# Where the first loads of x and of the key weights are issued, and new tables for the order, in a two-layer attention and gated-layer kernel

## The chip, the cores and the metric

The kernel runs on one core of a Trainium2 chip. The metric is the device time of one execution in microseconds (us); smaller is better. Engines are named TensorE (PE in the profile), VectorE (DVE), ScalarE (ACT), GpSimd (POOL) and SyncE (SP). PEld is TensorE's weight load.

## What is computed

The input x has 2048 rows of 512 values in bf16. Two blocks are applied in turn, and the pair is applied twice with the same weights:

```python
x = x + A(layernorm(x))     # attention, 32 heads of 16, causal window of 256 keys
x = x + B(layernorm(x))     # gated layer: (sigmoid(x @ w_gate) * (x @ w_up)) @ w_down, 1792 wide
x = x + A(layernorm(x))
x = x + B(layernorm(x))

def A(x):
    q, k, v = split(x @ wqkv)                      # per head
    s = (q @ k.T) / 4, where 0 <= i - j < 256
    return (softmax(s) @ v) @ wo
```

## The kernel before, in words

**Tiling.** Rows of x are cut into 16 tiles of 128 (`NT`), and four tiles make a group (`NTG` is 4 groups). All of x (`xsb`), all weights (`wq`, `wot`, `wg`, `wu`, `wd`) and all intermediate buffers lie in SBUF for the whole run. Within a tile, the rows lie in an interleaved manner over the partitions (two halves z of 64 rows), which is why one tile is loaded either as two DMAs of 64 partitions or as one DMA over a rearranged source.

**Stages of a tile.** The layer norm (`layer_norm`) takes statistics on VectorE (`stats`: L589, L590, and L592 for the first group), an inverse root on GpSimd (`root`: L598, L599) and applies both on VectorE (L617) into a buffer `xn`, of which there are two. The first tiles are transposed by TensorE (L638) and copied by ScalarE or VectorE (the shared helper `copy`, L666 on ScalarE and L668 on VectorE) into `xnT`; later tiles by a DMA transpose. Then `q_unit` (L703), `k_unit` (L734) and `v_unit` (L770) are matmuls with `wq`. The keys are evacuated (L666 or L668) and then split by a mask into even and odd heads on VectorE (L749, with `rms`). A visit of `scores` (L1029, L1040) writes four PSUM banks `Sps`, one exponential of 2048 columns on ScalarE (L1082) reads them into `PTring` or `edge`, VectorE multiplies masks in (L960), and `values` (L1109) multiplies with the values in `Vaug` and with copies of them, `Vl` and `Vh`, in which the two halves of a tile are swapped to other partitions and the rest is zero. Those copies are made by SP's DMAs (L1314, `half_values`). `zeros(z, i)` clears the rest of a copy (L534, GpSimd). After the values come the normalisation, the output projection (`oproj_unit`, L893, added to x at L899), the second norm, the gate and up projections (`glu_units`, L798, with a tanh at L816 and a product at L824) and the down projection (`down_units`, L862, added at L871). Rows of the result go out by SP's DMAs (L878).

**How the order is made.** No loop order is written down. While the program is built, a planner (`Plan`) plays the engines forward with costs in nanoseconds. Each piece of work is a task with its engine or a choice of engines, what it waits for, and a priority; whenever an engine is free in the plan, the ready task of lowest priority number is put next into that engine's instruction stream. TensorE's next piece is chosen by `pick` and `rank`: a score visit when the pace allows (`PACE`), else values, else a unit of matmuls. The tables `PRIO`, `SLACK`, `RANK` and their `LATE_` forms, `PACE` and `OPT` are plain numbers that set this order; `EXP_NS`, `SWITCH`, `COLD`, `RATE`, `LAND` and the like are what the planner believes of the hardware. On the chip, each engine runs its stream in that order, and semaphores hold an instruction until its inputs are there. The planner's numbers therefore change the order and nothing else.

**The gated layer's groups.** `GLU[0][OPT["g0"]]` and `GLU[1][OPT["g2"]]` say how many tiles of a layer share one pass over gate and up weights. A group of n tiles makes matmuls of n x 128 columns. In layer 0 both kernels use 1, 1, 1, 1, 2, 2, 4, 4.

**The first loads.** `loads` issues, on the queues SP and ACT, each tile of x as two halves: tile 0, tile 1, tiles 2 and 3; then the key weights, the query weights (each as two halves), and the value weights on ACT; then, on SP, tiles 4 to 7, `wot`, tiles 8 to 11, `wg`, `wu` and the rest (issues at L455). `constants` runs before that on GpSimd and VectorE: the identity for the transposes (L507, L508), parts of the value buffers (`ones`, L528 and L529), the masks `rms`, and the clears of `Vl`. `later_constants` makes masks, the clears of `Vh` and the rest as tasks of the plan. `keep_warm` (L1292) puts four matmuls on the identity into TensorE's stream where nothing else is ready.

Of the kernel before, what the change touches and what calls it, by code (L numbers as in the profile page):

```python
# [12 lines left out]
P = 128  # L13
S, D, H, DH, F = 2048, 512, 32, 16, 1792
# [42 lines left out]
def pool_ns(n):  # L57
# [4 lines left out]
TAIL = (384, 128)  # L62
GLU = [[[1] * 4 + [4], [1] * 4 + [2] * 2, [1] * 6 + [2], [1] * 8, [2] * 4, [1] * 2 + [2] * 3, [2] * 2 + [4]], [[4] * 3 + [2, 1, 1], [4] * 3 + [2, 2], [4] * 4]]
PACE = [2682, 3207, 1600, 2511, 23.52]
EARLY = 12
FILL = 800
# [3 lines left out]
PE_LATENCY = 180  # L70
COLD = 5200
SWITCH = 96
LAND = 1230
RATE = ((3300, 330.0), (5300, 160.0), (1e9, 345.0))
FIRST = 1100
# [5 lines left out]

PRIO = dict(st_x0=7.13, ap_x0=2.72, xt_x0=3.36, st_x1=-0.44, ap_x1=1.86, xt_x1=6.58, st_x=18.87, ap_x=6.56,
    xt_x=2.0, st_p=7.13, ap_p=4.46, xt_p=0.81, st_g=2.23, ap_g=1.32, xt_g=6.14, st_g0=5.97, ap_g0=3.21,
    xt_g0=1.33, tp=5.75, tp_g=-0.06, q=4.0, q0=5.51, q1=4.74, k=1.95, k0=-0.89, k1=-1.49, s=-1.15, s0=5.46,
    s1=3.28, v=0.28, v0=5.43, v1=14.72, vv=5.53, exp=3.64, exp0=4.71, m0=4.61, m00=-0.56, e0=1.11, e00=1.28,
    e1=7.21, e10=6.56, m2=0.64, m20=3.6, th=5.12, mu=-0.12, dn=1.29, add=-0.27, add0=1.8, out=-2.4, mv=5.8,
    mv0=6.23, oq=-2.27, oq0=-0.14, no=4.71, no0=2.61, on=5.93, on0=0.59, vc=9.2, vc0=-0.87)
OPT = dict(gu='SP', g1=1, bk=3, bq=2, wide=0, r0=2, g0=1, g2=1, x0=1, eps=1, hold=0, own=1, ck=0, cq=2,
    turn=2)
SLACK = dict(xt=1208, oq=843, on=211, vc=1208)  # L90
RANK = dict(tp=-1.708, o=-2, lead=14.747, far=7.411, v=9.3, g=1.778, d=1.823, feed=11.672, x3=21097, wd=474,
    go=364)
LATE_PRIO = dict(st_p=-0.04, ap_p=7.96, xt_p=-0.99, st_x=1.07, ap_x=4.81, xt_x=-1.16, st_g=1.75, ap_g=1.19,
    xt_g=2.76, q=3.84, k=4.33, s=4.05, v=0.61, exp=1.12, m0=4.62, e0=2.79, e1=4.39, m2=5.49, th=1.65, mu=2.51,
    dn=2.1, add=0.69, out=0.45, mv=3.49, oq=0.77, no=6.44, on=2.16, vc=0.22)
LATE_SLACK = dict(xt=489, oq=1327, on=2346, vc=897)
LATE_RANK = dict(tp=-2, o=1.576, lead=9.722, far=6.159, v=1.796, g=1.769, d=3.896, feed=7.551, go=1418)

# [69 lines left out]
class Plan:  # L168
# [20 lines left out]
    def at(self, time, fn=None):  # L189
        self.seq += 1  # L190
        heapq.heappush(self.heap, (time, self.seq, fn))
# [177 lines left out]
class Net:  # L369
# [74 lines left out]
    def loads(self, A_x, wqkv, wo, w_gate, w_up, w_down):  # L444
# [26 lines left out]
        def both(parts):  # L471
            done = Event()
            when_all(parts, done.fire)
            return done

        for t, n in {1: ((0, 1), (1, 1), (2, 2)), 2: ((0, 2), (2, 2)), 3: ((0, 1), (1, 3))}[OPT["x0"]]:
            ev = load_x(self.xsb[:, t:t + n, :], slice(t, t + n), n, 0, ("SP", "ACT"))
            for i in range(t, t + n):
                self.has_x[i] = ev
        if OPT["wide"]:  # L480
            self.has_wq["q"] = self.has_wq["k"] = both([
                load(self.wq[:, k:k + 2, 0:2 * D], wq_src[:, k:k + 2, 0:2 * D], 4 * P * D * 2, prio=0, queue=q, row=4 * D)
                for k, q in ((0, "ACT"), (2, "SP"))])
        else:
            for w in "kq":
                h = slice("qk".index(w) * D, ("qk".index(w) + 1) * D)
                self.has_wq[w] = both([load(self.wq[:, k:k + 2, h], wq_src[:, k:k + 2, h], 2 * P * D * 2, prio=0, queue=q)
                                       for k, q in ((0, "ACT"), (2, "SP"))])
        self.has_wq["v"] = load(self.wq[:, :, 2 * D:3 * D], wq_src[:, :, 2 * D:3 * D], D * D * 2, prio=0, queue="ACT")
        x_group(1)  # L490
# [12 lines left out]

    def constants(self):
        nc = self.nc
        nc.gpsimd.memset(self.nhalf[:], -0.5)
        nc.gpsimd.memset(self.ident[:], 0.0)  # L507
        nc.gpsimd.affine_select(out=self.ident[:], in_=self.ident[:], compare_op=ALU.not_equal, fill=1.0,  # L508
                                base=0, pattern=[[-1, P]], channel_multiplier=1)
        for i in range(2):  # L510
            self.ones(i, nc.vector)
        nc.vector.memset(self.rms[0][:], 0.0)
        for m in range(4):
            nc.vector.memset(self.rms[0][32 * m:32 * m + 16, :], 1.0)
        nc.vector.tensor_scalar(out=self.rms[1][:], in0=self.rms[0][:], scalar1=-1.0, scalar2=1.0,
                                op0=ALU.mult, op1=ALU.add)
        for i in range(2):
            self.zeros(0, i)
        self.pl.free["POOL"] = 3000.0
        self.pl.free["SP"] = self.pl.free["ACT"] = 750.0  # L520
        self.pl.at(750.0)
        self.pl.at(1500.0)
        self.pl.free["DVE"] = 3600.0
        self.pl.at(3600.0)

# [10 lines left out]
    def later_constants(self):  # L536
# [11 lines left out]
        def mask2(e):  # L548
            for z in range(2):
# [8 lines left out]
                                    op0=ALU.mult, op1=ALU.add)  # L558

        for i in range(2):  # L560
            self.vzero[i] = pl.task({"POOL": 800}, lambda e, i=i: self.zeros(1, i), first, prio=8, port=True).done
# [7 lines left out]
    def layer_norm(self, key, t, deps):  # L569
# [50 lines left out]
        if key == ("p", 0, 0) and t >= 2 and OPT["hold"]:  # L620
            deps = deps + [self.applied[t - 2]]
        a = pl.task({"DVE": 910 + 70 * first}, stats, deps, self.prio["st_" + kind], lambda: "st" in box or self.has("st"))
        if not alone:
# [378 lines left out]
    def scores(self, L, t, kind, i):  # L1002
# [5 lines left out]
        if kind == "A":  # L1008
# [23 lines left out]
            runs = cut  # L1032
            return pl.count(8 * len(runs)) or 220
        if kind == "R":
            zs = range(2 if t + 2 < NT else 1)
            for z in zs:
                for cq in range(NCQ):
                    q0, o = ((L * NT + t) * 2 + 5 * z) % (QG * TGW // HP) * HP, (z * NCQ + cq) * HP
                    for m in range(4):
# [3 lines left out]
                                         start=True, stop=True, tile_position=(32 * m, 0))  # L1043
            return pl.count(16 * len(zs)) or 122 * len(zs)
        for cq in range(NCQ):
            for e in range(2):
                o = (2 * cq + e) * HP
                q0 = ((L * NT + t) * 2 + 1) % (QG * TGW // HP) * HP
                for m in range(4):
                    nc.tensor.matmul(self.sps[:, m, o:o + HP], lhsT=kTp[32 * m:32 * m + 32, cq, tt, e, :],  # L1050
                                     rhs=self.qT[32 * m:32 * m + 32, cq, q0:q0 + HP],
                                     start=True, stop=True, tile_position=(32 * m, 0))
        return pl.count(32) or 230

# [29 lines left out]
    def values(self, L, t, half, bank):  # L1084
# [7 lines left out]
        for col in range(4):  # L1092
# [10 lines left out]
            for k, (where, Va, p) in enumerate(parts):  # L1103
# [8 lines left out]
                pl.count(4)  # L1112
        return n * 56

# [173 lines left out]
    def keep_warm(self, bank):  # L1288

        nc, pl = self.nc, self.pl  # L1290
        for i in range(4):
            nc.tensor.matmul(self.banks[bank][:, 0:P], lhsT=self.ident[:], rhs=self.ident[:], start=True, stop=True)  # L1292
        pl.count(4)
        pl.matmul("d", 4 * 56)
# [8 lines left out]
    def half_values(self):  # L1303
# [18 lines left out]
        for z in range(2):  # L1322
            some = pairs if z == 0 else [k for k in pairs if k[1] + 2 < NT]
            for i, (L, t) in enumerate(some):
                V = self.Vaug[(L * NT + t) // 2 % VP]
                deps = [self.v_ready[L, t], self.v_ready[L, t + 1]]
                if z and i < 2:
                    deps.append(self.vzero[i])
                if i >= 2:
# [83 lines left out]
    def go(self, *srcs):  # L1413
# [28 lines left out]
        self.pv_list = [k + (h,) for k in LT for h in range(2)]  # L1442
        self.constants()
        self.loads(*srcs)
        self.streams = [[], [], [], [], []]
        self.roots, self.pairs, self.vones, self.vzero = {}, {}, {}, {}
        self.applied = [Event() for _ in range(NBG)]
# [74 lines left out]
```

The softmax here doesn't subtract the row's maximum and nothing guards it: scores larger than these inputs give would overflow.

## Time and profile before

| | |
|---|---|
| median of 3 runs | 541.69 us (541.08 to 543.02) |
| span of the profiled execution, first to last instruction | 539.6 us |
| what the median has beyond that span | 2.1 us |
| TensorE busy, instructions | 531.1 us, 9658 matmuls |
| VectorE busy | 420.5 us |
| ScalarE busy | 382.3 us |
| GpSimd busy | 43.4 us |
| mean granted TensorE clock | 0.999 |

The profile gives the span of one execution; for that execution no other total is given, so the median of the runs stands beside it. Busy time of a pipelined engine counts as busy whatever overlaps, so 98% on TensorE doesn't say that it works at its peak. In the timeline a row with a count (x10) joins instructions of one kind that follow one another; its length runs from the first start to the last end. What stands in square brackets is the engine's idle time before it and what ended that.

### The profile page before, as it was taken

The numbers are of one execution on the slowest core, as the hardware profiler recorded it, in microseconds if no ns is written. First come the engines' busy times: TensorE is split into PE (matmuls) and PEld (weight loads), VectorE is DVE, ScalarE is ACT, GpSimd is POOL, SyncE is SP. The second block draws the span as 40 slices with busy tenths as digits, with TensorE's granted clock in tenths as the row PEclk, the third lists the DMA queues.
The fourth block names the chain that finished last, engine by engine and source line by source line (L and its number), as shares of the span: only waits on it lengthen the run. The fifth ranks groups of instructions, "written<-read, shape, count | busy, mean of one in ns | idle before, by whom it ended". The sixth has DMA issues, their size and how long they took to land.

```text
span 539.6 us, 21359 instructions
## 1 busy us (share of the span) xinstructions
PE 531.1 (98%) x9658; PEld 293.0 (54%) x9658; DVE 420.5 (78%) x844; ACT 382.3 (71%) x380; POOL 43.4 (8%) x99
## 2 busy tenths in 40 slices
PE   8999999999999999999999999999999999999997
PEld 8446755855767444544444444544444444455873
DVE  6999999789878997798977789778677785674442
ACT  4989989878888687776778767787667866540330
POOL 5301110001000110101100010101000000000000
PEclk9999999999999999999999999999999999999999
DMA  8890334232421323143110622117211241132001
GB/s 260 317 227 15 43 72 57 50 61 63 72 52 33 72 51 60 36 101 59 32 35 14 105 51 47 38 42 108 54 45 28 60 72 50 24 70 58 2 11 39
DMA packets 95067, 36.23 MB, mean 67 GB/s; under 512 B 78336, under 2 KB 93952, under 8 KB 94976
## 3 DMA queue, kind: packets, MB, share of 16 engines
q1 hardware_dynamic: 93600, 33.56, 29.9%
q8 instruction: 75, 1.23, 1.0%
q10 hardware_dynamic: 1376, 1.31, 0.8%
q14 instruction: 16, 0.13, 0.1%
HBM read 9.70 MB, written 2.10 MB: 22 GB/s over the span
## 4 chain that ended last, share of the span: by engine, by line
PE 89%; DVE 5%; ACT 2%; DMA 1%; issue 1%; POOL 0%; SPq 0%; ACTq 0%; POOLq 0%
PE bank L798 37%; PE bank L862 18%; PE bank L1109 9%; PE Sps L1029 7%; PE bank L893 5%; PE bank L734 4%; PE bank L770 3%; PE bank L703 3%; PE Sps L1040 2%; ACT PTring L1082 1%; DMA wq<-in_A_wqkv_dram 1%; DVE kTp L749 1%; DVE st L589 1%; DVE PTring L960 1%; DVE edge L960 1%
## 5 line engine op out<-in xcount | busy, mean ns | idle before, releaser
L1082 ACT ACTIVATE PTring<-Sps 128x2048 bf16<-128x2048 f32 (+1 forms) x122 | 226.0, 1852 | 63.2 <-PE Sps L1029 59.2
L798 PE MATMUL bank<-xnT,wu 128*128 128x512 bf16 (+2 forms) x728 | 128.2, 297 | 0.0
L798 PE MATMUL bank<-xnT,wg 128*128 128x512 bf16 (+2 forms) x728 | 128.2, 298 | 0.0
L862 PE MATMUL bank<-wd,hT 128*128 128x512 bf16 (+2 forms) x462 | 109.9, 373 | 0.0
L824 DVE SCALAR_TENSOR_TENSOR hT<-hT,bank 128x256 bf16<-128x256 bf16 (+1 forms) x154 | 80.8, 537 | 34.0 <-ACT hT L816 21.2
L816 ACT ACTIVATE hT<-bank 128x256 bf16<-128x256 f32 (+1 forms) x154 | 71.1, 482 | 48.5 <-PE bank L798 47.8
L798 PEld LDWEIGHTS <-wg 128*128 128x128 bf16 x728 | 60.7, 98 | 36.7 <-issue 2.3
L798 PEld LDWEIGHTS <-wu 128*128 128x128 bf16 x728 | 61.4, 98 | 34.5 <-issue 2.5
L1082 ACT ACTIVATE edge<-Sps 128x2048 bf16<-128x2048 f32 (+1 forms) x32 | 56.6, 1770 | 17.3 <-PE Sps L1040 17.3
L862 PEld LDWEIGHTS <-hT 128*128 128x128 bf16 x462 | 43.0, 98 | 46.4 <-issue 2.2
L668 DVE CAST OTs<-bank 128x512 bf16<-128x512 f32 x59 | 43.0, 729 | 21.5 <-PE bank L1109 21.1
L960 DVE TENSOR_TENSOR PTring<-PTring,mask 128x1024 bf16<-128x1024 bf16 x64 | 43.7, 684 | 12.3 <-ACT PTring L1082 12.1
L1109 PE MATMUL bank<-PTring,Vaug 128*32 128x64 bf16 (+1 forms) x2880 | 52.0, 203 | 0.0
L1109 PEld LDWEIGHTS <-Vaug 128*32 128x32 bf16 x2880 | 44.0, 97 | 12.0 <-issue 10.4
L1029 PE MATMUL Sps<-qT,kTp 32*128 32x256 bf16 (+3 forms) x1216 | 47.4, 248 | 1.2 <-ACT PTring L1082 1.1
L598 POOL TENSOR_SCALAR st<-st 128x2 f32<-128x2 f32 (+1 forms) x33 | 10.7, 325 | 443.6 <-DVE st L590 443.6
L589 DVE BATCH_NORM_STATS2 st<-xsb 128x6 f32<-128x512 bf16 x64 | 43.9, 686 | 1.7 <-DMA xsb<-in_A_x_dram 1.2
L1109 PE MATMUL bank<-edge,Vl 128*32 128x64 bf16 x1024 | 44.4, 193 | 0.1
L960 DVE TENSOR_TENSOR edge<-edge,maske 128x1024 bf16<-128x1024 bf16 x60 | 40.3, 682 | 3.4 <-ACT edge L1082 3.3
L1029 PEld LDWEIGHTS <-kTp 32*128 32x128 bf16 x1216 | 18.2, 92 | 45.4 <-issue 43.5
L1109 PE MATMUL bank<-edge,Vh 128*32 128x64 bf16 x896 | 40.8, 193 | 0.0
L960 DVE TENSOR_TENSOR PTring<-PTring,maskn 128x1024 bf16<-128x1024 bf16 x56 | 38.2, 682 | 0.0
(73 smaller groups left out, 522.0 us busy)
## 6 DMA issues: line engine op xcount, KB each, us to landing
Vl<-Vaug SPq DMA_DIRECT2D x32, 68.0 KB, 2.4
out_dram<-xsb SPq DMA_DIRECT2D x15, 128.0 KB, 2.1
Vh<-Vaug SPq DMA_DIRECT2D x28, 68.0 KB, 2.5
wg<-in_B_w_gate_dram SPq DMA_DIRECT2D x2, 896.0 KB, 9.7
wu<-in_B_w_up_dram SPq DMA_DIRECT2D x2, 896.0 KB
wd<-in_B_w_down_dram SPq DMA_DIRECT2D x7, 256.0 KB, 5.3
xsb<-in_A_x_dram SPq DMA_DIRECT2D x6, 256.0 KB, 7.4
wq<-in_A_wqkv_dram ACTq DMA_DIRECT2D x2, 256.0 KB, 4.5
```

The lines of the kernel that those rows point to most:

```text
L589: nc.vector.bn_stats(out=st[:, 0:6], in_=self.xsb[:, t, :])
L668: self.nc.vector.tensor_copy(out=out, in_=in_)
L734: return [(mm_ns(w), lambda kt=kt, o=o: nc.tensor.matmul(self.banks[bank][:, o:o + w], lhsT=self.wq[:, kt, D + cq * P:D + cq * P + P], rhs ...
L798: return [(mm_ns(w), lambda i=i, j=j, fc=fc, wt=wt, kt=kt: self.nc.tensor.matmul(pt[:, i, j, :], lhsT=wt[:, kt, fc * P:(fc + 1) * P], rhs= ...
L816: self.nc.scalar.activation(out=self.hT[:, ch[0] * GW:ch[0] * GW + size], in_=pt, func=AF.Tanh, scale=0.5)
L824: self.nc.vector.scalar_tensor_tensor(out=h, in0=h, scalar=1.0, in1=pt, op0=ALU.add, op1=ALU.mult)
L862: nc.tensor.matmul(self.banks[bank][:, 0:w], lhsT=self.hT[:, at:at + P], rhs=self.wd[:, fc, d], start=fc == 0, stop=fc == FC - 1)
L893: return [(mm_ns(D), lambda c=c: nc.tensor.matmul(self.banks[bank][:], lhsT=b[0][:, c, :], rhs=self.wot[:, c, :], start=c == 0, stop=c == ...
L960: done = pl.task({"DVE": dve_bf_ns(1024)}, lambda e: nc.vector.tensor_tensor(out=r, in0=r, in1=m.to_broadcast([P, 16, HP]), op=ALU.mult), ...
L1029: nc.tensor.matmul(self.sps[:, m, o:o + n * HP], lhsT=kTp[32 * m:32 * m + 32, i, tt, e, :], rhs=self.qT[32 * m:32 * m + 32, i, q0:q0 + n * ...
L1082: nc.scalar.activation(out=out, in_=src, func=AF.Exp, scale=scale)
L1109: nc.tensor.matmul(o, lhsT=Va[:, c0:c0 + 32], rhs=p(h), start=k == 0 or t == 0, stop=k == len(parts) - 1 or t == 0, tile_position=(0, 32 * g))
```

## The change

Five things are done.

1. The first loads are issued in another order and on three queues. SP issues half of tile 0, half of the key weights, tile 3, half of the query weights; ACT issues the other halves of tile 0, of the key weights and of the query weights, and the value weights. Tiles 1 and 2 are issued by GpSimd as its first instructions, in `constants`. The plan takes fixed landing times for all of these (`ARRIVE`) in place of a rate.
2. The clears of the two `Vl` buffers are no longer in `constants` but tasks of the plan after the norm of tile 3 (`lzero`), on GpSimd; the copies into them wait for them.
3. The constant `nhalf` and the zeros under the identity are written by VectorE; VectorE also clears 128 columns of `hT`, and the keep-warm matmuls multiply these instead of the identity.
4. `OPT["hold"]` is 1: the statistics of tiles 2 and 3 wait until the application of tiles 0 and 1 has begun, in the plan.
5. The tables have new numbers, and some costs of the planner too. Among them, the last layer's gated groups are 4, 4, 4, 4 where they were 4, 4, 4, 2, 2.

```diff
-GLU = [[..., [1] * 4 + [2] * 2, ...], [..., [4] * 3 + [2, 2], ...]]
-PACE = [2682, 3207, 1600, 2511, 23.52]
-EARLY = 12
+GLU = [[..., [1, 1, 1, 1, 2, 2], ...], [..., [4, 4, 4, 4], ...]]
+PACE = [2704.38, 2914.32, 405.77, 1639.67, 24.53]
+EARLY = 8
...
-COLD = 5200
-SWITCH = 96
+ARRIVE = dict(x0=3150, x1=4300, x2=5200, x3=5900, k=6100, q=7700, v=9300)
+COLD = 6000
+SWITCH = 100
...
-RATE = ((3300, 330.0), (5300, 160.0), (1e9, 345.0))
+RATE = ((9000, 40.0), (1e9, 345.0))
...
-PRIO = ...
+PRIO = ...
-OPT = dict(..., hold=0, ...)
+OPT = dict(..., hold=1, ...)
-SLACK = dict(xt=1208, oq=843, on=211, vc=1208)
+SLACK = dict(xt=200, oq=79, on=315, vc=4034)
...
@@ loads
-        for t, n in {1: ((0, 1), (1, 1), (2, 2)), ...}[OPT["x0"]]:
-            ev = load_x(self.xsb[:, t:t + n, :], slice(t, t + n), n, 0, ("SP", "ACT"))
...
-            for w in "kq":
-                h = slice("qk".index(w) * D, ("qk".index(w) + 1) * D)
-                self.has_wq[w] = both([load(self.wq[:, k:k + 2, h], ..., queue=q)
-                                       for k, q in ((0, "ACT"), (2, "SP"))])
-        self.has_wq["v"] = load(self.wq[:, :, 2 * D:3 * D], ..., queue="ACT")
+        def at(name, parts):
+            done, landed = Event(), Event()
+            pl.at(ARRIVE[name], landed.fire)
+            when_all(parts + [landed], done.fire)
+            return done
+
+        def first(dst, src, queue):
+            q = {"SP": nc.sync, "ACT": nc.scalar}[queue]
+            t = pl.task({queue: 650}, lambda e: q.dma_start(out=dst, in_=src), (), 0)
+            return t.done
+
+        self.has_x[0] = at("x0", [first(self.xsb[z:P:2, 0, :], x_src[z][:, 0, :], ("SP", "ACT")[z]) for z in range(2)])
+        self.has_x[1] = at("x1", [])
+        self.has_x[2] = at("x2", [])
+        for w in "kq":
+            h = slice("qk".index(w) * D, ("qk".index(w) + 1) * D)
+            self.has_wq[w] = at(w, [first(self.wq[:, k:k + 2, h], wq_src[:, k:k + 2, h], q) for k, q in ((0, "SP"), (2, "ACT"))])
+            if w == "k":
+                self.has_x[3] = at("x3", [first(self.xsb[:, 3, :], ..., "SP")])
+        self.has_wq["v"] = at("v", [first(self.wq[:, :, 2 * D:3 * D], wq_src[:, :, 2 * D:3 * D], "ACT")])
@@ constants
-        nc.gpsimd.memset(self.nhalf[:], -0.5)
-        nc.gpsimd.memset(self.ident[:], 0.0)
+        for t in (1, 2):
+            nc.gpsimd.dma_start(out=self.xsb[:, t, :], in_=x_src[t])
+        nc.vector.memset(self.hT[:, 0:P], 0.0)
+        nc.vector.memset(self.nhalf[:], -0.5)
+        nc.vector.memset(self.ident[:], 0.0)
...
-        for i in range(2):
-            self.zeros(0, i)
-        self.pl.free["POOL"] = 3000.0
+        self.pl.free["POOL"] = 4000.0
...
-        self.pl.free["DVE"] = 3600.0
+        self.pl.free["DVE"] = 3250.0
@@ later_constants
         for i in range(2):
+            self.lzero[i] = pl.task({"POOL": 800}, lambda e, i=i: self.zeros(0, i), first, prio=5.5, port=True).done
+        for i in range(2):
             self.vzero[i] = pl.task({"POOL": 800}, lambda e, i=i: self.zeros(1, i), first, prio=8, port=True).done
@@ keep_warm
-            nc.tensor.matmul(self.banks[bank][:, 0:P], lhsT=self.ident[:], rhs=self.ident[:], start=True, stop=True)
+            nc.tensor.matmul(self.banks[bank][:, 0:P], lhsT=self.hT[:, 0:P], rhs=self.hT[:, 0:P], start=True, stop=True)
@@ half_values
-                if z and i < 2:
-                    deps.append(self.vzero[i])
+                if i < 2:
+                    deps.append((self.lzero, self.vzero)[z][i])
```

The returned costs in `scores` (220 to 234, 122 to 126, 230 to 244), `values` (56 to 59.3 for each) and the statistics' cost in `layer_norm` (70 to 190 more for the first group) are the planner's alone.

## The prediction

> **What bounds the kernel now.** I read the page's busy rows by slice first, then the windows, then the timeline of the first 14 us. The three engine rows of the page, 40 slices of 13.5 us:
>
> ```profile
> PE   8999999999999999999999999999999999999997
> DVE  6999999789878997798977789778677785674442
> ACT  4989989878888687776778767787667866540330
> ```
>
> TensorE is full from the second slice to the last but one. So time can be lost only at the two ends or in how TensorE spends its busy time. The windows (columns: window, its length, then busy us and count of PE, PEld, DVE, ACT, POOL, then clock, DMA share, GB/s) split the front at its events:
>
> ```profile
> 0.00:3.28 3.28, 1.83 (x18) 1.84 (x19) 0.67 (x11) 0.00 (x0) 2.13 (x13) 1.00 0.25 68
> 3.28:8.58 5.30, 4.61 (x55) 4.44 (x53) 4.85 (x15) 2.46 (x3) 2.32 (x4) 1.00 0.94 288
> 8.58:13.48 4.90, 4.82 (x81) 4.56 (x81) 3.59 (x12) 3.08 (x6) 2.84 (x14) 1.00 1.09 360
> 13.48:30.00 16.52, 15.32 (x179) 7.07 (x178) 15.90 (x38) 15.29 (x20) 6.09 (x15) 1.00 0.87 308
> 30.00:47.00 17.00, 16.74 (x273) 7.97 (x271) 16.31 (x35) 15.85 (x13) 1.53 (x3) 1.00 0.67 133
> ...
> 47.00:85.00 38.00, 37.87 (x988) 25.65 (x986) 36.20 (x80) 33.86 (x35) 4.06 (x8) 1.00 0.28 49
> 85.00:490.00 405.00, 403.56 (x7737) 208.99 (x7736) 323.52 (x616) 300.98 (x279) 23.47 (x42) 1.00 0.29 55
> ```
>
> Until 8.58 x and weights are awaited and the PE count is mostly keep-warm matmuls. From 13.48 to 47 VectorE (32.2 of 33.5 us) and ScalarE (31.1) set the pace together. After that TensorE does. Now TensorE's and SyncE's timelines of the front, and VectorE's split before the first scores:
>
> ```profile
> 3.02 1.14 SPq L455 DMA_DIRECT2D wq<-in_A_wqkv_dram  x2
> 7.62 0.28 PE L734 MATMUL bank<-xnT,wq 128*128 128x128 bf16 x2
> 8.58 0.73 PE L734 MATMUL bank<-xnT,wq 128*128 128x128 bf16 x10 [0.69 <-DMA wq<-in_A_wqkv_dram]
> 9.43 0.39 PE L638 MATMUL Sps<-ident,xn 128*128 128x128 bf16 x4
> 10.49 0.38 PE L638 MATMUL Sps<-ident,xn 128*128 128x128 bf16 x4
> 12.65 1.39 DVE L749 TENSOR_SCALAR kTp<-kTp,rm 128x512 bf16<-128x512 bf16 x4 [0.58 <-ACT kTp L666]
> 13.49 0.40 PE L1029 MATMUL Sps<-qT,kTp 32*128 32x256 bf16 x8
> ```
>
> The second half of the key weights is SP's fourth DMA; it is issued at 3.02 and its piece in the chain is 5.51 us. TensorE's K matmuls run out of weights at 7.9 and stand until 8.58. The transpose of tile 2 is behind them in TensorE's order: its input was ready at 8.40 (L617, 7.99 + 0.41), it runs at 9.43. Everything up to the first scores follows that.
>
> **What the Trainium skill says.** "DMA: Bandwidth & Descriptors", section "Issuing engines are not separate DMA queues": another issuing engine saves only the sequencer's issue time. The trace fits: SP's and ACT's loads take about 0.6 us each to issue, one behind the other, while the DMA engines are at 0.94 of their time from 3.28 on. Section "Anatomy of one DMA" of the same page gives a GpSimd DMA about 2.0 us plus bytes/436e3; no run here shows one. "SBUF — State Buffer", section "SBUF: two separate sides": VectorE and GpSimd exclude one another on a shared port, and a GpSimd DMA needs it for its descriptors. The trace has such a case: L551 on 64 columns takes 1.28 us beside GpSimd memsets, L553 on the same shape 0.34. "TensorE: Matmul & The Clock Gate", section "Back-to-back issue gap": N/2.4 + 2.5 ns. Here four matmuls of 512 columns come every 0.87 us, of 256 every 0.44, as the formula says.
>
> **The change part by part.**
>
> *Order of loads.* SP's issues before the key weights fall from three (x0, x1, x2-3) to one, ACT's likewise. With 0.6 us per issue the SP half goes from 3.02 to about 1.45. It then shares the engines with x0, x1, x2 and its other half: 128 + 256 + 512 KB, where before some 1.7 MB in all had moved by its landing at 8.5. In the timeline of DMA rates the core had moved about 0.9 MB by 6.0 us; that is an estimate of the landing of K, and close to the 6.1 us that the new plan writes for it. K is then no longer late: the first K matmul waits for tile 0's transposed copy (6.70 + 0.59 = 7.29). Next late is tile 2's norm. Step by step with present durations: transpose of tile 2 at 8.45 (0.39), copy 0.59, to 9.45; transpose of tile 3 at 9.3 (L617 ends 9.25), copy behind, to 10.3; its four K matmuls 0.3; evacuation L666 0.59, to 11.2; split L749 two of 0.36, to 12.0; scores at 12.1 instead of 13.49: **-1.4 us**. One catch: the mask arithmetic (L551 to L557) holds VectorE from 9.86 to 12.06 and was covered by the late K; if the order keeps it ahead of the split, 0.1 to 0.8 us come back. I take -1.2, ends -1.9 and +0.5.
>
> *Tiles 1 and 2 on GpSimd.* Two DMAs of 128 KB, not in the old trace. By the page, 2.0 + 0.3 us behind GpSimd's first free moment at 0.78: tile 1 lands at 3.1 at best. The plan assumes 4.3 and 5.2; the statistics of those tiles now start at 4.30 and 5.64. I take no cost. Ends: a gain of nothing, because tile 0's statistics hold VectorE until 4.37 anyway; a loss, if descriptors are held up, is the third rival's. Queued behind the two issues on GpSimd are only the identity's select and the first root (4.53); the plan has GpSimd free at 4.0.
>
> *Constants.* Three more memsets on VectorE (about 0.1 us each) lie in its idle 1.18 us before tile 0; keep-warm matmuls start on a cleared hT instead of the identity. Both 0; without that cover 0.3 us. The six clears of the V copies leave GpSimd's 1.34 to 2.95 and go behind the masks, at about 9.8; GpSimd had nothing from 11.6 to 15.0, and the first copies are issued at 21.21. 0, but up to +0.5 by the shared port. The statistics of tiles 2 and 3 now wait for the application of tiles 0 and 1: that is the order VectorE has today (5.32 before 5.64, 6.65 before 6.97), so 0.
>
> *Last group of the gated layer.* Layer 1's tiles 12 to 15 go from two groups of two to one of four. Timelines of both widths:
>
> ```profile
> 502.69 0.60 PE L798 MATMUL bank<-xnT,wg 128*128 128x256 bf16 x4
> 503.13 0.60 PE L798 MATMUL bank<-xnT,wu 128*128 128x256 bf16 x4
> ...
> 484.93 1.03 PE L798 MATMUL bank<-xnT,wg 128*128 128x512 bf16 x4
> 485.80 1.03 PE L798 MATMUL bank<-xnT,wu 128*128 128x512 bf16 x4
> ```
>
> 224 matmuls at 109 ns become 112 at 216: 24.4 - 24.2 = **-0.2 us**. The group now waits for tile 15; the down projections of tiles 8 to 10 (14 x 0.216 = 3.0 us each) cover that chain, which took 490.1 to 496.8. Without it up to +3. The last down matmuls and the 3.2 us behind them (536.4 to 539.6) stay.
>
> *New tables.* Work and precision stay; only the order moves. Bound from the trace, start of a matmul to start of the next, less the usual spacing and a change of mode (about 96 ns): 2.5 us of stalls from 13.5 to 47 and 3.8 us after (the largest 0.6 us at 140.5 and 0.5 at 90.9). Changes of mode, some 377 by 96 ns, are set by the 154 score visits and 64 value pairs. Layer 1's visits are paced at 2914 instead of 3207 ns: 77 x 0.29 = 22 us earlier end of attention, with the dense work behind it longer by as much, and no gain by itself. Of the 6.3 us I take a tenth: **-0.6**, ends -2.5 and +1.5.
>
> Sum: -1.2 - 0.2 - 0.6 = -2.0 on the span of 539.6, hence 537.6. The median of the runs is 541.69, which is 2.1 above that span; the forecast for the median is 539.6. A measurement of this kernel tells about 0.3% (1.6 us) from no change.
>
> **The rivals.**
> 1. *Front gained and kept* (forecast, chance 0.55): 539.6; own range 537.6 to 540.1.
> 2. *Front gained, then absorbed.* VectorE and ScalarE are the bound until 47; if tiles 4 to 7 land late (now 12.37 by x4's first statistics at 13.96, with only 1.6 us of room), or the mask arithmetic goes ahead of the split, the earlier scores are followed by a wait. For it: both engines at 95% there. Against it: their work isn't more, so a shift carries through. Gain 0 to 1.4: about 540.9. Chance 0.27. That the GpSimd load is just another hidden issue falls here.
> 3. *GpSimd's loads late* (slower, 0.10). Tile 1's statistics stand ahead of tile 0's application in VectorE's order. Landing after 4.3 is paid one for one: the 2.0 us gained are gone at 6.3, and at 7.9 the kernel is 0.3% slower; descriptors held up twice would do it. About 543.5. Against it: VectorE has only small memsets up to 3.28.
> 4. *Order searched well* (0.08): half of the 6.3 us of stalls goes as well: about 537.
>
> **How the numbers follow.** Faster by over 0.3%: nearly all of 1 less its upper edge (0.50) and 4 (0.08), 0.58. Within: the rest of 1 and most of 2, 0.30. Slower: 3 and a stalled end group, 0.12. The range 537.0 to 542.6 leaves out half of 3 and the far ends of 4.
>
> **What would show it.** Right: K landing by about 6.3, no TensorE wait for wq, tile 2's transpose near 8.5, first scores at 12 to 12.5, windows from 14 to 47 as full as before but ending earlier, attention's last exponential near 450 instead of 471, no PE gap after it. Wrong: first statistics of tile 1 after 5 us, a gap of VectorE there, first scores at 13.5 or later, or more than 6 us of stalls behind 13.5.

## The result, and the profile after

The changed kernel takes 542.08 us (median of 20 runs, 540.89 to 542.85) where the kernel before takes 541.42 (20 runs, 540.61 to 543.02). The ratio is 1.0006, 95% interval 0.9998 to 1.0013: no change that can be told, where -0.4% was the likeliest forecast. The profiled execution has a span of 539.7 us against 539.6.

Nothing moved in the sum, but the parts did. The same rows of the page (busy tenths in 40 slices):

```profile
PE   8999999999999999999999999999999999999997
DVE  5999989889798898778978878798867876543332
ACT  3999988878879786786878886787858774230320
```

Near the end VectorE and ScalarE fall off earlier: attention's last exponential starts at 452.98 us where the kernel before has 471.26, as the pace says. The windows of the changed kernel at the same cuts (window, length, busy us and count of PE, PEld, DVE, ACT, POOL, clock, DMA share, GB/s):

```profile
0.00:3.28 3.28, 2.24 (x22) 2.24 (x23) 0.86 (x14) 0.22 (x1) 1.97 (x7) 1.00 0.25 54
3.28:8.58 5.30, 4.08 (x39) 3.81 (x38) 3.59 (x11) 1.65 (x2) 1.33 (x3) 1.00 1.04 341
8.58:13.48 4.90, 4.79 (x70) 4.52 (x68) 3.57 (x14) 2.21 (x4) 3.87 (x14) 1.00 1.11 351
13.48:30.00 16.52, 15.39 (x194) 7.71 (x194) 15.28 (x37) 15.97 (x20) 6.80 (x22) 1.00 0.68 257
30.00:47.00 17.00, 16.32 (x284) 8.33 (x285) 16.61 (x37) 16.25 (x17) 1.79 (x5) 1.00 0.39 86
```

From 3.28 to 8.58 VectorE does 3.59 us of work where it did 4.85: the norms have fallen behind. The timeline of the changed kernel says why (start, length, engine, line, what; in brackets the idle time before and what ended it):

```profile
1.31 1.38 POOL L519 DMA_DIRECT2D xsb<-in_A_x_dram  x2 [0.82 <-POOLq L1522]
5.24 0.69 DVE L605 BATCH_NORM_STATS2 st<-xsb 128x6 f32<-128x512 bf16 x1 [0.86 <-DMA xsb<-in_A_x_dram]
6.25 0.41 DVE L633 TENSOR_SCALAR xn<-xsb,st 128x512 bf16<-128x512 bf16 x1
6.72 0.61 PE L654 MATMUL Sps<-ident,xn 128*128 128x128 bf16 x4 [1.23 <-DVE xn L633]
7.12 1.91 PE L1308 MATMUL bank<-hT 128*128 128x128 bf16 x16
7.30 0.69 DVE L605 BATCH_NORM_STATS2 st<-xsb 128x6 f32<-128x512 bf16 x1 [0.64 <-DMA xsb<-in_A_x_dram]
9.25 0.74 PE L750 MATMUL bank<-xnT,wq 128*128 128x128 bf16 x5
12.02 0.38 PE L654 MATMUL Sps<-ident,xn 128*128 128x128 bf16 x4
15.54 0.40 PE L1045 MATMUL Sps<-qT,kTp 32*128 32x256 bf16 x8
```

Tile 1 comes from GpSimd's queue and its statistics start at 5.24, not 4.30; tile 2's at 7.30, not 5.64. Tile 1's statistics stand ahead of tile 0's application in VectorE's order, so tile 0 is applied at 6.25 instead of 5.32. TensorE has run out of keep-warm matmuls and stands 1.23 us. It then still runs at half speed: the 16 keep-warm matmuls at 7.12 take 1.91 us, 119 ns each, where in the kernel before 16 of them took 1.06:

```profile
6.50 1.06 PE L1292 MATMUL bank<-ident 128*128 128x128 bf16 x16
```

(The clock record reads 1.00 here in both kernels. That these matmuls run at half clock is read from their spacing alone.) No K matmul waits for weights any more, as forecast, but the first runs only at 9.25. In TensorE's order it stands behind the transpose of tile 1, whose application (8.32 instead of 6.65) came behind the late statistics of tile 2. The first scores start at 15.54, not 13.49.

Yet two exponentials later most of that is gone. The third exponential (the first into `edge`) in the kernel before and in the changed kernel:

```profile
21.39 1.88 ACT L1082 ACTIVATE edge<-Sps 128x2048 bf16<-128x2048 f32 x1 [0.25 <-PE Sps L1040]
```

```profile
21.91 1.88 ACT L1098 ACTIVATE edge<-Sps 128x2048 bf16<-128x2048 f32 x1
```

The first exponential was 2.2 us late, the third is 0.5 us late. Two readings were open: the front is absorbed by engines that are full anyway, or the new tables win back what the new loads lose.

### The profile page after: what moved, and what is told of

Read it like the earlier page. It is cut to its first block, busy times and chain, and to the rows that moved or that the text cites. A ratio compares the mean times of both kernels' runs of the same rounds, so it can differ in the third digit from the quotient of the medians.

```text
span 539.7 us, 21042 instructions
## 1 busy us (share of the span) xinstructions
PE 524.8 (97%) x9468; PEld 281.7 (52%) x9538; DVE 415.2 (77%) x830; ACT 380.9 (71%) x369; POOL 42.4 (8%) x99
## 4 chain that ended last, share of the span: by engine, by line
PE 84%; DVE 9%; DMA 3%; issue 2%; ACT 1%; POOL 1%; DVEq 0%; ACTq 0%; POOLq 0%
PE bank L814 37%; PE bank L878 16%; PE bank L1125 8%; PE Sps L1045 6%; PE bank L909 4%; PE bank L719 4%; PE bank L750 3%; PE bank L786 3%; DMA xnT<-xn 3%; DVE kTp L765 2%; PE Sps L1056 2%; DVE st L605 1%; DVE PTring L976 1%; DVE xn L633 1%; DVE OTs L684 1%
## 5 line engine op out<-in xcount | busy, mean ns | idle before, releaser
L814 PE MATMUL bank<-xnT,wu 128*128 128x512 bf16 (+2 forms) x672 | 125.0, 308 | 0.4 <-issue 0.2
L814 PE MATMUL bank<-xnT,wg 128*128 128x512 bf16 (+2 forms) x672 | 123.7, 309 | 1.0 <-DMA xnT<-xn 1.0
L840 DVE SCALAR_TENSOR_TENSOR hT<-hT,bank 128x512 bf16<-128x512 bf16 (+1 forms) x140 | 78.6, 575 | 45.8 <-PE bank L814 37.6
L832 ACT ACTIVATE hT<-bank 128x512 bf16<-128x512 f32 (+1 forms) x140 | 69.4, 516 | 60.1 <-PE bank L814 59.9
L878 PE MATMUL bank<-wd,hT 128*128 128x512 bf16 (+2 forms) x427 | 102.5, 372 | 3.0 <-issue 1.8
L814 PEld LDWEIGHTS <-wu 128*128 128x128 bf16 x672 | 55.9, 98 | 40.0 <-issue 2.3
L814 PEld LDWEIGHTS <-wg 128*128 128x128 bf16 x672 | 55.2, 98 | 41.1 <-issue 2.9
L614 POOL TENSOR_SCALAR st<-st 128x2 f32<-128x2 f32 (+1 forms) x33 | 9.0, 274 | 423.7 <-DVE st L606 423.7
```

Of the source, the lines that this page charges most:

```text
L814: return [(mm_ns(w), lambda i=i, j=j, fc=fc, wt=wt, kt=kt: self.nc.tensor.matmul(pt[:, i, j, :], lhsT=wt[:, kt, fc * P:(fc + 1) * P], rhs= ...
L832: self.nc.scalar.activation(out=self.hT[:, ch[0] * GW:ch[0] * GW + size], in_=pt, func=AF.Tanh, scale=0.5)
L840: self.nc.vector.scalar_tensor_tensor(out=h, in0=h, scalar=1.0, in1=pt, op0=ALU.add, op1=ALU.mult)
L878: nc.tensor.matmul(self.banks[bank][:, 0:w], lhsT=self.hT[:, at:at + P], rhs=self.wd[:, fc, d], start=fc == 0, stop=fc == FC - 1)
```

## The experiments

The first four cross loads and tables. In each, TensorE and VectorE keep their instructions in the order of the kernel that it starts from; only the DMAs of the first loads are exchanged. Where GpSimd issues nothing, tiles 1 and 2 stand ahead of K, so K is not second on its queue.

**New tables, tiles 1 and 2 on the hardware queues.**

```diff
-        for t in (1, 2):
-            nc.gpsimd.dma_start(out=self.xsb[:, t, :], in_=x_src[t])
...
+            def fn(e):
+                q.dma_start(out=self.xsb[z:P:2, 0, :], in_=x_src[z][:, 0, :])
+                q.dma_start(out=self.xsb[:, 1 + z, :], in_=...[1 + z])   # z = 0: SP, 1: ACT
```

> The changed kernel in its own order on TensorE and VectorE, with tiles 1 and 2 issued by SP and ACT right behind tile 0 instead of by GpSimd. Every theory: tile 1 landed by 4.3 us and tile 2 by 5.5, key weights by 7.0, first exponential near 13 instead of 16.1. Theory A (late GpSimd loads cost the front one for one, and the tables had won it back): 1.5 to 2.2 us faster than the changed kernel, 540.0 to 540.5. Theory B (the front is absorbed: the third exponential was only 0.5 us later in the changed kernel though the first was 2.2 later, so VectorE and ScalarE set the pace until 47 us): within 0.6 us of the changed kernel, 541.5 to 542.1.

Measured: 542.36, ratio to the kernel before 1.0017 (1.0009 to 1.0026). Neither theory had foreseen it: the first scores came later still, at 16.83. Its TensorE timeline:

```profile
7.38 0.44 PE L755 MATMUL bank<-xnT,wq 128*128 128x128 bf16 x5
10.04 0.40 PE L724 MATMUL bank<-xnT,wq 128*128 128x128 bf16 x4 [2.22 <-DMA wq<-in_A_wqkv_dram]
16.83 0.40 PE L1050 MATMUL Sps<-qT,kTp 32*128 32x256 bf16 x8
```

and its windows, with the granted clock in the third column from the end:

```profile
10.90:14.30 3.40, 3.40 (x36) 3.40 (x34) 1.60 (x7) 1.36 (x3) 2.29 (x11) 0.50 1.12 361
14.30:17.00 2.70, 2.70 (x42) 1.98 (x40) 1.47 (x5) 2.31 (x6) 0.00 (x0) 1.00 1.01 400
```

Tiles 1 and 2 were in time (statistics at 4.34 and 5.67), and with that tile 3 and the query weights were late. TensorE's order has query matmuls of tile 0 early, stood 2.22 us for them, and then was granted half its clock for 3.4 us. Not every execution has that stretch: of the 22 runs, 10 have a mean granted clock under 0.998 and a median of 543.1 us, the other 12 have 541.4.

**New tables, loads as before.**

```diff
+        x0 = [several(("SP", "ACT")[z], [half(0, 1, z), half(1, 1, z), half(2, 2, z)]) for z in range(2)]
...
+        self.has_wq["k"] = at("k", [several(q, [weights("k", k)]) for k, q in ((2, "SP"), (0, "ACT"))])
```

> The changed kernel in its own order, with all first loads on SP and ACT in the order of the kernel before (tile 0, tile 1, tiles 2 and 3, K, Q, V). Key weights land at 8.5 again, so TensorE waits for them. Theory A: first exponential near 14, 1 to 1.5 us faster than the changed kernel, 540.6 to 541.1, and slower than with K second on those queues by 0.5 or more. Theory B: within 0.6 us of the changed kernel.

Measured: 540.82, ratio 0.9997 (0.9985 to 1.0009). By the runs it can't be told from the kernel before, nor, with overlapping intervals, from the changed kernel (1.0006, 0.5 us more). Its trace is what bears on the two readings. The third exponential:

```profile
20.71 1.88 ACT L1110 ACTIVATE edge<-Sps 128x2048 bf16<-128x2048 f32 x1
```

The table puts the start of four events side by side (us, from the timelines; one execution each):

| | first scores | third exponential | 25th | TensorE's last matmul ends |
|---|---|---|---|---|
| before | 13.49 | 21.39 | 78.66 | 536.35 |
| old tables, new loads | 14.47 | 22.41 | 79.46 | 536.79 |
| new tables, old loads | 14.35 | 20.71 | 77.79 | 535.02 |
| after (both new) | 15.54 | 21.91 | 78.98 | 536.23 |

With the new tables, the new loads cost 1.2 us at the first scores and the same at the third exponential, at the 25th and at the end. That is theory A's carry, one for one; theory B's absorption didn't happen in these traces. The tables alone make the first scores 0.86 later and the third exponential 0.68 earlier: the first scores are no yardstick for a change of order. One execution each is thin ground for a difference between rows: the last run below (the pace alone) has the first loads and the front of the kernel before, and its first scores came 0.54 us earlier. The carry from column to column doesn't suffer from that.

**Old tables, new loads.** The tasks of the old plan keep place and cost; their DMAs are replaced.

```diff
...
+        slots = {"SP": [[half(0, 0)], [weights("k", 0)], [whole(3)], [weights("q", 0)], []],
+                 "ACT": [[half(0, 1)], [weights("k", 2)], [weights("q", 2)], [value_weights()], [], []]}
...
+        for t in (1, 2):
+            nc.gpsimd.dma_start(out=self.xsb[:, t, :], in_=x_src[t])
         nc.gpsimd.memset(self.nhalf[:], -0.5)
         nc.gpsimd.memset(self.ident[:], 0.0)
```

> The kernel before in its own order, with the first loads issued as in the changed kernel: tiles 1 and 2 by GpSimd ahead of its constants, K second on SP and ACT. Tile 1 lands at 5.2 and tile 2 at 7.3, the identity waits on GpSimd for both issues, and keep-warm matmuls on it start later. First exponential near 16. Theory A: slower than before by 1.5 to 2.2 us, 543.0 to 543.6. Theory B: within 0.6 us of before, 541.4 to 542.0.

Measured: 542.1, ratio 1.0015 (1.0009 to 1.0022), 0.8 us slower. The front is 1.0 us late up to the third exponential, 0.8 at the 25th, and 0.45 at TensorE's end: between the two theories. Statistics of tile 1 start at 5.58, of tile 2 at 7.33. Here the identity too waits on GpSimd for the two issues, so the keep-warm matmuls start at 3.38 instead of 1.45; the 1.0 us are not the loads' alone.

**Old tables, K ahead of tile 3, nothing on GpSimd.** As the run before, with tile 1 behind tile 0 on SP and tile 2 on ACT.

> The kernel before in its own order, with tile 0, then tile 1 on SP and tile 2 on ACT, then K, tile 3, Q and V, nothing on GpSimd. Key weights land near 7 instead of 8.5, x as before. First exponential near 12.7 instead of 13.9 unless TensorE's order keeps it. Theory A: faster than before by 0.8 to 1.4 us, 540.0 to 540.6. Theory B: within 0.5 us of before.

Measured: 541.8, ratio 1.0009 (1.0001 to 1.0017): not faster. K came earlier, but the statistics of tile 3 start at 8.16 instead of 6.97, behind this wait, and the first scores at 13.97 instead of 13.49. TensorE's last matmul ends at 536.3, as before: in this trace the 0.5 us lost in the front are won back by the end.

```profile
8.16 0.69 DVE L615 BATCH_NORM_STATS2 st<-xsb 128x6 f32<-128x512 bf16 x1 [0.69 <-DMA xsb<-in_A_x_dram]
```

The next runs ask what TensorE's clock has to do with it.

**More keep-warm matmuls where the first of these runs stood.** (From new tables with tiles 1 and 2 on the hardware queues, the first run above; 10 ahead of the first transpose, 30 ahead of the first query matmul.)

```diff
+        for i in range(self.extra.pop(u.name[0], 0)):
+            nc.tensor.matmul(self.banks[7][:, 0:P], lhsT=self.hT[:, 0:P], rhs=self.hT[:, 0:P], start=True, stop=True)
         fn()
...
+        self.extra = {'tp': 10, 'q': 30}
```

> The kernel with the changed order whose tiles 1 and 2 come from SP and ACT (its TensorE stood 2.2 us for the query weights and then ran at half clock from 10.9 to 14.3 us), with 10 more keep-warm matmuls ahead of the first transpose and 30 ahead of the first query matmul; nothing else moves. Theory C (TensorE's clock decides the front): full clock from 10 to 17 us, first scores near 15.2 instead of 16.8, and the whole kernel 1.2 to 1.8 us faster than without them, 540.6 to 541.2. Theory D (the late x and query weights decide, the clock is a side effect): first scores within 0.4 us of 16.8, time within 0.5 us of 542.4.

Measured: 540.17, ratio 0.9971 (0.9961 to 0.9982), faster than both kernels by some 0.3%. Full clock in both windows where the run without them stood or was slow:

```profile
7.80:10.80 3.00, 2.51 (x39) 2.22 (x39) 1.37 (x4) 0.59 (x1) 1.04 (x3) 1.00 1.06 360
10.90:14.30 3.40, 3.29 (x57) 3.16 (x58) 2.06 (x9) 1.64 (x4) 2.68 (x12) 1.00 1.10 363
```

57 matmuls in the window that held 36. The size was right and even too small, the place only in part: the first scores came at 16.27, not 15.2 (in this execution the loads were later: tile 3's statistics at 8.93 instead of 8.47). The third exponential is 0.56 us earlier than without the added matmuls, TensorE's end 1.7 us (535.36 against 537.07). Where the other 1.1 us come from, the profile shows in part: the run without them stood 0.36 and 0.21 us for DMA transposes at 124.6 and 205.8, this one didn't. The same holds wider: all five traces with the new tables and no added matmuls show such stands (0.8 to 1.8 us in all), the five with added matmuls show none. Why is open, and so is how much of the 0.46% between the two ratios is the clock: the 12 runs without added matmuls whose clock was full have a median of 541.4, still 1.2 us above 540.17.

**The same for the changed kernel itself**, 12 matmuls ahead of its first transpose.

> The changed kernel as it is, with 12 more keep-warm matmuls ahead of its first transpose, where its TensorE stood 1.2 us at half clock. Theory C: full clock from about 6 us instead of 10.4, first scores 0.4 to 0.8 us earlier than 15.53, time 0.5 to 1 us lower, 541.1 to 541.6, and a narrower spread of runs. Theory D: the front waits for tiles 1 and 2 and for the query weights anyway, first scores within 0.2 us and time within 0.3 us of the changed kernel.

Measured: 541.58, ratio 0.9999 (0.9991 to 1.0007) to the kernel before. By the spacing of its matmuls TensorE is at full clock from about 6 us instead of 10.4, and the first scores come at 15.55 where the changed kernel has 15.54:

```profile
7.07 1.06 PE L1310 MATMUL bank<-hT 128*128 128x128 bf16 x16
15.55 0.40 PE L1045 MATMUL Sps<-qT,kTp 32*128 32x256 bf16 x8
```

That is theory D for this front: the late tiles set the chain, and half clock was the consequence. For the whole time theory D isn't borne out. The median lies in theory C's range and the spread became narrower (541.1 to 542.0), as theory C said. Of the changed kernel's 20 runs, 7 have a mean granted clock of 0.997 (median 542.2 us), the other 13 have 0.999 or 1.000 (541.4); of the 13 runs with added matmuls none is under 0.999. So the clock does fall in some executions of the changed kernel, which its one trace doesn't show, and the added matmuls went with its not falling. A gain beyond the noise isn't shown: 0.9999 and 1.0006 have overlapping intervals.

**The same for the new tables with old loads**, with 4, 10 and 8 matmuls.

> The changed order with the loads as before on SP and ACT, and 4, 10 and 8 more keep-warm matmuls where its TensorE stood (first transpose, first key matmul, first query matmul). It was at full clock already in its profile, so theory C and D both leave the profile's first scores at 14.35 within 0.2 us; theory C expects the runs above 541.4 to go (they would be runs whose clock fell in those waits), so a median of 540.0 to 540.5 and 0.1 to 0.2% faster than the kernel before. Theory D: median within 0.3 us of 540.8.

Measured: 543.4, ratio 1.0025 (1.0012 to 1.0039), against both theories. The front is 0.46 us later, but the larger loss is far from the edit. Timeline of TensorE and of SP's queue:

```profile
455.05 1.76 SPq L1164 DMA_TRANSPOSE OnT<-On  x1
455.10 0.21 PE L1137 MATMUL bank<-PTring,Vaug 128*32 128x64 bf16 x4
457.85 0.25 PE L1137 MATMUL bank<-edge,Vl 128*32 128x64 bf16 x4 [2.54 <-issue]
```

TensorE stood 2.54 us ("issue" means that it waited for nothing that the profile shows), and the clock record falls to half from 457.7 to 461.1. Of its 8 runs, 5 have a mean granted clock under 0.998. In the trace one transfer on the instruction queue runs from 454.96 to 456.36, while SP issues a DMA transpose at 455.05. I took it that 22 more matmuls had moved the place in TensorE's stream where a fetch falls, onto that transpose, and tried another number.

**12 added matmuls instead of 22.**

> The changed order with the loads as before and 4, 4 and 4 more keep-warm matmuls instead of 4, 10 and 8. The run with 22 had a stand of 2.5 us on TensorE at 455 us, where an instruction fetch and a DMA transpose were issued together. Theory F (the place of the fetches in the stream decides, and 22 moved them onto that transpose): no stand over 1 us after 440, time 540.0 to 540.9. Theory G (the added matmuls themselves cost the front): 542 or more, with first scores at 14.8.

Measured: 540.94, ratio 0.9991 (0.9985 to 0.9998). The longest stand after 440 us is 0.88 us (at 457.4, "issue" again), and the first scores at 14.90 are as late as with 22. So the added matmuls hardly cost, and theory F holds as far as this goes: the long stand went with the number. That the transpose is what held the fetch was not tried.

**The last group in twos.**

```diff
-GLU = [..., [[4, 4, 4, 2, 1, 1], [4, 4, 4, 4], [4, 4, 4, 4]]]
+GLU = [..., [[4, 4, 4, 2, 1, 1], [4, 4, 4, 2, 2], [4, 4, 4, 4]]]
```

> The changed kernel with the last layer's groups back at 4, 4, 4, 2, 2. The order up to the last group stays. By the count of matmuls (224 of 256 columns at 109 ns against 112 of 512 at 216) it is 0.2 us slower than the changed kernel, 542.1 to 542.4; if the group of four made TensorE wait for tile 15, it is faster by the length of that wait, which should then show as a gap behind the last output projection.

Measured: 542.02, ratio 1.0009 (1.0002 to 1.0015) to the kernel before; the changed kernel's is 1.0006. The medians can't tell 0.2 us. In the profiles, the stretch from the last exponential's start to TensorE's end takes 83.46 us in twos (453.64 to 537.10) and 83.26 in fours (452.98 to 536.23; 83.26 again in three other traces with fours). That is the forecast's 0.2, but not proof of its cause: with 12 matmuls added in the front and the groups left in fours, the same stretch takes 84.01. No gap stands behind the last output projection.

**Only tile 2 on GpSimd.** (From the run that reached 540.17, tile 1 in halves on SP and ACT.)

> The changed order with 10 and 30 more keep-warm matmuls (as the run that reached 540.17), tile 1 in two halves on SP and ACT right behind tile 0, and only tile 2 on GpSimd. Tile 1 lands by 4.3 us; tile 2, alone on GpSimd, lands at 5.2 as tile 1 did there. If the second GpSimd load is what comes too late, K lands by 7, Q by 9.7, first scores near 15.5 instead of 16.3, and the time is 539.5 to 540.2. If any GpSimd load holds the front, first scores at 16.3 or later, 540.2 to 541.

Measured: 540.02, ratio 0.9979 (0.9969 to 0.9989); first scores at 15.99, tile 2's statistics at 5.87 without a wait. As good as the run without GpSimd and no better within the intervals: one GpSimd load, for a tile that is needed later, does no harm that these runs can tell. Faster than the changed kernel by about 0.3%.

**The planner told the landings that the trace shows.**

```diff
-ARRIVE = dict(x0=3150, x1=4300, x2=5200, x3=5900, k=6100, q=7700, v=9300)
+ARRIVE = dict(x0=3200, x1=5200, x2=7300, x3=7750, k=6150, q=9800, v=9900)
```

> The changed kernel with its loads, where the planner is told the landings that its trace shows (x1 5200, x2 7300, x3 7750, k 6150, q 9800, v 9900) instead of the assumed ones, so that TensorE has the key matmuls of tiles 0 and 1 ahead of any query matmul. Theory H (the order fits the wrong landings and TensorE's order holds the front): first scores 14.5 to 15.0 instead of 15.53, third exponential 0.5 us earlier, time 541.3 to 541.7. Theory I (the landings themselves hold it): first scores within 0.3 us, and the time moves only by what the rest of the order does, up to 1 us either way.

Measured: 549.53, ratio 1.0152 (1.0138 to 1.0165). Theory I for the front (first scores 15.65, third exponential 21.84), but "up to 1 us" for the rest was far off: in the traces 1.7 us are lost by the 25th exponential, won back by the 78th (225.57 against 225.91), and 9.2 us are lost from there to the end (319.6 against 310.3 us), with stands such as 1.8 us for a DMA transpose at 377. In the traced execution TensorE also ran at half clock from 48.1 to 51.5. The tables were fitted to the choices that the planner makes with the old inputs; with truer inputs it makes others, and here the tables served them worse.

**The pace of layer 2 alone, in the kernel before.** (Layer 1 where counted from 0.)

```diff
-PACE = [2682, 3207, 1600, 2511, 23.52]
+PACE = [2682, 2914.32, 1600, 2511, 23.52]
```

> The kernel before with the pace of the second layer's visits at 2914 ns instead of 3207, nothing else. Attention ends about 20 us earlier and the dense work behind it is longer by as much. My account: no gain by itself, within 0.5 us of before. The rival: the tables' gain of the second layer (the changed kernel needs 310.3 us from the 78th exponential to TensorE's end, the kernel before 311.9) comes from that pace, so 1.0 to 1.5 us faster.

Measured: 542.51, ratio 1.002 (1.0013 to 1.0028). Attention's last exponential starts at 452.01 instead of 471.26, and the kernel is 1.1 us slower; from the 78th exponential to TensorE's end it takes 312.9 us, 1.0 more than before. The rival falls, and so does "no gain by itself, within 0.5 us": by itself the pace costs. Whether it pays together with the other numbers was not tried.

## Why the prediction was right or wrong, point by point

- **Range and chances.** 542.08 lies in 537.0 to 542.6, but by luck: the likeliest case, faster by 0.4%, didn't come, and three of the four signs that were to show the forecast wrong came (tile 1's statistics at 5.24, VectorE's gap of 0.86 us before them, first scores at 15.54). What came is "within 0.3%", by another way than case 2: the front wasn't gained and absorbed, it was lost. The traces say that the tables won it back; the runs can't confirm a gain of that size. The forecast also added 2.1 us to the span; over the runs the time beyond the span is 1.7 us for the changed kernel and 2.0 for the kernel before, and why wasn't looked for.
- **Order of loads, -1.2: the step that failed.** K did land in time for TensorE, but it was no longer what the front waited for. I had priced K's way from its own row and had left x where it was. Tiles 0 to 3 of x, K and Q are 1.5 MB on the same DMA engines, which run at full share from 3.3 us on; putting K ahead put tile 3 or the query weights later. Where K was early and GpSimd out of it (old tables), the kernel was 0.09% slower, not 0.2% faster. The term was also too large even for a K that comes in time. In the trace of the run with the pace alone, with the loads as before, K happened to be in time for TensorE:

```profile
7.87 0.91 PE L734 MATMUL bank<-xnT,wq 128*128 128x128 bf16 x12
12.95 0.40 PE L1029 MATMUL Sps<-qT,kTp 32*128 32x256 bf16 x8
```

  The first scores came at 12.95, 0.54 us earlier and not 1.4. The page of the Trainium skill that I drew on ("DMA: Bandwidth & Descriptors", section "Issuing engines are not separate DMA queues") says that DMAs of all issuing engines run on the same 16 DMA engines and interleave; the forecast used it for the third queue but not for the order.
- **Tiles 1 and 2 on GpSimd, no cost: the second step that failed.** The landing of tile 1 was taken from the plan's own table (4.3). The trace has 3.90 us from issue to landing in the chain, to 5.2:

```profile
1.31 3.90 DMA xsb<-in_A_x_dram
5.24 0.70 DVE st L605
```

  The same page's section "Anatomy of one DMA" would give 2.3 us, an estimate; here key loads were in flight beside it. The third rival's mechanism is thus what happened in the front, at 5.2 instead of its 6.3: tile 0 is applied 0.93 us later (6.25 against 5.32), as much as tile 1's statistics are late, and tile 1 1.67 us later (8.32 against 6.65), as much as tile 2's are. Whether its descriptors were held up or its packets only shared the DMA engines with the key loads was not tried. What GpSimd's part alone costs the whole kernel isn't shown either. The crossing exchanges order and queue together, and the runs with and without GpSimd are 1.0015 and 1.0009 with the old tables, 1.0006 and 1.0017 with the new.
- **TensorE's clock: not in the prediction.** A later tile 0 left TensorE idle while it still ran at half speed, until 10.4 us. In the traces of the changed kernel, filling that gap moved the first scores by nothing. Its variant without GpSimd loads went from 1.0017 to 0.9971 with added matmuls, but of the 1.7 us between the two traces only 0.56 lie in the front; the rest lies behind the 25th exponential and isn't explained.
- **New tables, -0.6: in the range, not shown.** With old loads, the medians give a gain of 0.3 us, and by the interval anything from a gain of 0.8 to a loss of 0.5; the one pair of profiled executions gives a gain of 1.3.
- **No TensorE gap behind attention's last exponential: right.** From 452.98 to the end the trace shows no stand over 0.25 us. The changed order does have stands further ahead, at 123.4, 204.3 and 366.2, for DMA transposes of `xnT` (0.3, 0.7 and 0.4 us); the kernel before stands nowhere that way. Whether more than 6 us of stalls lie behind 13.5, as the last sign asked, can't be counted: this trace has 9468 matmuls for 9538 weight loads, so records are missing.
- **Last group, -0.2: 0.20 in the profiles**, in a stretch that 12 matmuls elsewhere moved by more. Attention's end: 453 where 450 was expected.
- **Constants, 0: no cost seen.** The clears run from 11.43 to 13.15, not from about 9.8, and the first copies are issued at 22.1, well behind them. The mask row that took 1.28 us takes 0.29.

## What to carry to other kernels

When loads that share the DMA engines are reordered, price the landing of the last of them that the front needs, not of the one that is moved forward; here every load put ahead made another late. Judge a change of order by an event behind the phase that it reorders (here the third exponential), and cross it with the other edits before crediting either. And look at the granted clock of every run, not of the traced one alone: here it fell in a third of the runs of the changed kernel, and its trace shows nothing of it. Tables that were fitted to one course of a planner (one sequence of its choices) may serve another badly; in the one run here it cost 1.5%.

## What the runs showed of the hardware

- A GpSimd load of 128 KB took 3.9 us from issue to landing beside the key loads. The second, issued by 2.7, showed almost no packets until 5.7 (1 packet of that queue from 4.8 to 5.7 against 48 in the next 1.1 us).
- TensorE, at full clock, stood from 7.8 to 10.0 us and was granted half its clock from 10.9 to 14.3, after the wait was over. The stretches of half clock in the other traces are as long: 457.7 to 461.1 and 48.1 to 51.5.
- A coincidence of an instruction fetch and a DMA transpose went with a stand of 2.5 us on TensorE and half clock for 3.4 us after it; with 12 instead of 22 matmuls added far ahead, the longest stand in that part was 0.88 us. One trace shows it, and the cause isn't shown.
